# Decode block on one core: 24 of w2's rows on VectorE, wo's rows in pairs over two column groups, and TensorE's program on a 256 boundary

## Chip, core and metric

The kernel runs on one core of a Trainium2 chip. The metric is the device time of one execution in microseconds (us). Engines: TensorE (PE, with PEld for its weight loads), VectorE (DVE), ScalarE (ACT), GpSimd (POOL) and SyncE (SP), which issues nearly all DMA transfers. Sixteen DMA engines share every transfer.

## The reference

One token x of 1024 elements goes through a layer norm, then through two branches whose results are added to x:

```python
xn = layernorm(x)
# A: attention of 32 query heads over the last 4096 positions of 4 KV heads, head size 128
q = xn @ wq                                   # 1024 x 4096
p = softmax(q . k * 128**-0.5)                # 8 query heads share one KV head
A = (p . v) @ wo                              # 4096 x 1024
# B: MLP
h = gelu_tanh(layernorm(xn) @ w1 + b1)        # 1024 x 3584
B = h @ w2 + b2                               # 3584 x 1024
out = x + A + B
```

All inputs are bf16. Weights and the cached keys and values that are used come to 39.86 MB.

## The kernel before

All operations are written down in one plan (class `Plan`, lines 15 to 124) that works out the semaphore waits between engines; each engine then runs its operations in the order in which they were added. A read after a write waits on VectorE too, except on TensorE, where order is enough.

SyncE issues the transfers in this order: the keys (4 x 1 MB, line 181), wq in two halves (240), b1, x and b2 (318 to 320), w1 in two halves (359, 360), the values in three pieces (364), w2 in two pieces of 14 rows (401, 402), wo's rows 0 to 15 in one piece (446), and rows 16 to 31 in pieces of 8, 4, 2, 1 and 1 rows (`cuts`, 447 to 449). A "row" of w2 or wo is a tile of 128 partitions x 1024 columns: partition p holds row p*28+c of w2 or p*32+c of wo. Four SBUF slots of 32 KB per partition are reused: a transfer waits until the slot's earlier reader is done.

Stages: layer norms (272 to 308) on VectorE with small matmuls; transposition of the keys by VectorE (329) and ScalarE with VectorE (334, 338); q = xn @ wq (355) in four column groups; scores (395); softmax (399 to 428); w1 (375) in two halves around the softmax; gelu (434) and its transposition into hT (438), where hT[:, c, 0] is the column of weights for w2's row c; attention output (444), its head selection o_m, o_f, o_bf (451 to 455) and the column form o8 (457 to 460).

The end: w2's 28 rows are multiplied on TensorE into PSUM tile accw (467 to 473), each row as two matmuls of 512 columns in two column groups (the result's two halves lie on partitions 0 and 32). VectorE adds x + b2 (475). wo's rows 0 to 27, the bulk, go the same way into qo_ps (483 to 488). VectorE adds the w2 result in two pieces of 192 and 320 columns (491, 492). The last four rows go into acc2 in pieces of 320 and 192 columns (493 to 503); after row 30 four fp32 matmuls with one contraction row bring the 192-column piece of the bulk into that accumulation:

```python
        if c == CWO - 2:
            for half in range(2):
                pr = 32 * half
                mm32(acc_b[pr:pr + 1, :], ones_f[pr:pr + 1, 0:1], bulk_b[pr:pr + 1, :], False, False, ...)
```

VectorE adds the 320-column piece and converts (509), ScalarE converts the other (510), and two transfers write the output (512, 513).

TensorE's operations stand in a block of their own (lines 106 to 118) that ends with a branch back to its start which is never taken; `branch_hint` names that branch at the block's head. A second such branch at the start (lines 188 to 196) waits for x and leads to a block behind the program.

Of the kernel before, what the change touches and what calls it, by code (L numbers as in the profile page):

```python
# [7 lines left out]
FP32 = mybir.dt.float32  # L8
BF16 = mybir.dt.bfloat16
ACT = mybir.ActivationFunctionType  # L10
ALU = mybir.AluOpType
# [3 lines left out]
class Plan:  # L15
# [11 lines left out]
    def emit(self, done, never, inner):  # L27
        nc, ops = self.nc, self.ops
# [28 lines left out]
        for n, (eng, fn, r, w, dma, _) in enumerate(ops):  # L57
            c, mine = clock[eng], []
# [26 lines left out]
        def put(n):  # L85
            eng, fn, r, w, dma, _ = ops[n]
            lanes = {}
            for m in waits[n]:
                s, v = value[m]
                if id(s) not in lanes or lanes[id(s)][1] < v:  # L90
                    lanes[id(s)] = (s, v)
            for s, v in lanes.values():
                self.engines[eng].wait_ge(s, v)
            i = fn()
            if i is not None and n in value:
                i.then_inc(value[n][0], value[n][1] if dma is not None else 1)

        for n, o in enumerate(ops):
            if o[0] != "pe":
                put(n)  # L100
# [3 lines left out]
        only = [mybir.EngineType.PE]  # L104
        pe = nc.tensor
        pe_ops = [n for n, o in enumerate(ops) if o[0] == "pe"]
        pe.br("pe_main")
        nc.enter_bb("pe_main", valid_engines=only)
        back = pe.mark_branch_hint_location()
        for n in pe_ops:  # L110
            put(n)
        pe.br_eq(never, 1, "pe_main", "pe_last").branch_hint(back)
        nc.enter_bb("pe_last", valid_engines=only)
        pe.br("pe_end")
        nc.enter_bb("pe_far", parent=inner, valid_engines=only)
        pe.nop()
        pe.br("pe_go")
        nc.enter_bb("pe_end", valid_engines=only)
        pe.nop()
# [3 lines left out]
def kernel(  # L123
# [14 lines left out]
    nc = tc.nc  # L138
# [16 lines left out]
    TAIL = 4  # L155
    NA = 320
    NH = Fd // 8
# [4 lines left out]
    def sb(name, shape, dt):  # L162
        return nc.alloc_sbuf_tensor(name, shape, dt).ap()

    def ps(name, shape):
        return nc.alloc_psum_tensor(name, shape, FP32).ap()
# [5 lines left out]
    accw = ps("accw", [P, 512])  # L172
# [10 lines left out]

    x32 = sb("x32", [Hq, Hq], BF16)
# [4 lines left out]
    with tc.tile_critical():  # L189
        never = nc.tensor.alloc_register("pe_never")  # L190
        nc.tensor.reg_mov(never, 0)
        inner = nc.cur_bb
        far = nc.tensor.mark_branch_hint_location()
        nc.tensor.wait_ge(x_sem, 16)
        nc.tensor.br_eq(never, 1, "pe_far", "pe_go").branch_hint(far)
        nc.switch_bb("pe_go")
# [6 lines left out]
    def op(eng, fn, r=(), w=()):  # L203
        plan.add(eng, fn, r, w)

    def dma(eng, out_ap, in_ap, r=(), w=(), over=()):
        q = plan.engines[eng]
        plan.add(eng, lambda: q.dma_start(out=out_ap, in_=in_ap), r, w, True, over)  # L208

    def ldw(w_ap, pos, r):  # L210
        def go():
            with nc.discard():
                i = pe.ldweights(w_ap, tile_position=pos).ins
            return pe.add_instruction(mybir.InstLdweights(  # L214
                name=nc.get_next_instruction_name(), engine=i.engine, tile_size=(P, 32), tile_position=pos, ins=i.ins, outs=i.outs))
        op("pe", go, r, ())

    def mm(out_ap, w_ap, x_ap, start, stop, pos, r, w):
        def go():
            with nc.discard():  # L220
                i = pe.matmul(out_ap, lhsT=w_ap, rhs=x_ap, start=start, stop=stop, tile_position=pos).ins
            return pe.add_instruction(mybir.InstMatmult(  # L222
                name=nc.get_next_instruction_name(), engine=i.engine, start_tensor_calc=start, stop_tensor_calc=stop,
                tile_size=i.tile_size, tile_position=i.tile_position, ins=i.ins, outs=i.outs, ldweights=False))
        op("pe", go, r, w)
# [43 lines left out]
    op("dve", lambda: dve.memset(accw[0:33, :], 0.0), (), ("accw",))  # L269
# [43 lines left out]
    x2 = sb("x2", [33, 512], BF16)  # L313
    b2x = sb("b2x", [33, 512], BF16)
    b1x = sb("b1x", [P, 2 * NH], BF16)
    for name, t in (("x2", x2), ("b2x", b2x), ("b1x", b1x)):
        op("pool", lambda t=t: pool.memset(t, 0.0), (), (name,))
    dma("sp", b1x[0:97:32, :], B_b1.rearrange("(t n) -> t n", t=4), (), ("b1x",))
    dma("sp", x2[0:33:32, :], x_flat.rearrange("(t n) -> t n", t=2), (), ("x2",))
    dma("sp", b2x[0:33:32, :], B_b2.rearrange("(t n) -> t n", t=2), (), ("b2x",))  # L320

# [79 lines left out]
    dma("sp", slot[3][:, :14 * D].rearrange("p (r n) -> p r n", r=14), w2_v[:, 0:14, :], (), ("w20",), kt_srcs)  # L401
    dma("sp", slot[1][:, :14 * D].rearrange("p (r n) -> p r n", r=14), w2_v[:, 14:28, :], (), ("w21",), ("slot1",))
# [13 lines left out]
    op("dve", lambda: dve.tensor_scalar_mul(out=nmx, in0=mc_ps, scalar1=-scale), ("misc",), ("nmx",))  # L416
    l_loc = sb("l_loc", [P, 1], FP32)
# [17 lines left out]
    xb = sb("xb", [33, 512], FP32)  # L435
    op("dve", lambda: dve.tensor_tensor(out=xb, in0=x2, in1=b2x, op=ALU.add), ("x2", "b2x"), ("xb",))
    hT = sb("hT", [P, CW2, 32], BF16)
    op("dve", lambda: dve.transpose(out=hT, in_=h_sb.rearrange("p (d c) -> p c d", c=CW2)), ("h_sb",), ("hT",))

# [15 lines left out]
    op("dve", lambda: dve.tensor_copy(out=o_bf, in_=o_f), ("o_f",), ("o_bf",))  # L455
    o8_ps = misc[:, 160:192]
# [3 lines left out]
    op("dve", lambda: dve.tensor_copy(out=o8, in_=o8_ps), ("misc",), ("o8",))  # L460
    accf = qo_ps
    op("dve", lambda: dve.memset(accf, 0.0), (), ("qo",))
    acc_a, acc_b = acc2[:, 0, 0:NA], acc2[:, 1, 0:512 - NA]
    op("dve", lambda: dve.memset(acc2[:, :, 0:NA], 0.0), (), ("acc_a", "acc_b", "acc2"))


    for c in range(CW2):
        i, r = divmod(c, 14)
        wap = slot[3 - 2 * i][:, r * D:(r + 1) * D]
        for half in range(2):  # L470
            ldw(hT[:, c, 0:1], (0, 32 * half), ("hT",))
        for half in range(2):
            mm(accw[32 * half:32 * half + 1, :], hT[:, c, 0:1], wap[:, 512 * half:512 * half + 512], c == 0, c == CW2 - 1, (0, 32 * half), (f"w2{i}",), ("accw",))
    base = sb("base", [33, 512], FP32)
    op("dve", lambda: dve.tensor_tensor(out=base, in0=accw[0:33, :], in1=xb, op=ALU.add), ("accw", "xb"), ("base",))  # L475
    n_bulk = CWO - TAIL

    def wo_row(c):
        i, r = divmod(c, 16)
        key = "wo0" if i == 0 else f"wo1{max(a for a in cuts if a <= r)}"  # L480
        return wo_t[i][:, r, :], key

    for c in range(n_bulk):
        wap, key = wo_row(c)
        for half in range(2):
            ldw(o8[:, c:c + 1], (0, 32 * half), ("o8",))
            mm(accf[32 * half:32 * half + 1, :], o8[:, c:c + 1], wap[:, 512 * half:512 * half + 512],
               c == 0, c == n_bulk - 1, (0, 32 * half), (key,), ("qo",))
    bulk_b = sb("bulk_b", [33, 512 - NA], FP32)
    bulk_a = sb("bulk_a", [33, NA], FP32)  # L490
    op("dve", lambda: dve.tensor_tensor(out=bulk_b, in0=accf[0:33, NA:512], in1=base[:, NA:512], op=ALU.add), ("qo", "base"), ("bulk_b",))  # L491
    op("dve", lambda: dve.tensor_tensor(out=bulk_a, in0=accf[0:33, 0:NA], in1=base[:, 0:NA], op=ALU.add), ("qo", "base"), ("bulk_a",))
    for c in range(n_bulk, CWO):
        wap, key = wo_row(c)
        first, last = c == n_bulk, c == CWO - 1
        for half in range(2):
            ldw(o8[:, c:c + 1], (0, 32 * half), ("o8",))
        for half in range(2):
            pr, h0 = 32 * half, 512 * half
            mm(acc_a[pr:pr + 1, :], o8[:, c:c + 1], wap[:, h0:h0 + NA], first, last, (0, pr), (key,), ("acc_a",))  # L500
        for half in range(2):
            pr, h0 = 32 * half, 512 * half
            mm(acc_b[pr:pr + 1, :], o8[:, c:c + 1], wap[:, h0 + NA:h0 + 512], first, last, (0, pr), (key,), ("acc_b",))
        if c == CWO - 2:
            for half in range(2):
                pr = 32 * half
                mm32(acc_b[pr:pr + 1, :], ones_f[pr:pr + 1, 0:1], bulk_b[pr:pr + 1, :], False, False, ("ones_f", "bulk_b"), ("acc_b",), (pr, pr))
    res = sb("res", [33, 512], BF16)
    op("dve", lambda: dve.tensor_tensor(out=res[:, 0:NA], in0=acc_a[0:33, :], in1=bulk_a, op=ALU.add), ("acc_a", "bulk_a"), ("res_a",))  # L509
# [4 lines left out]
    plan.emit([len(plan.ops) - 2, len(plan.ops) - 1], never, inner)  # L514
# [30 lines left out]
```

## Time and profile before

Three runs: median 102.48 us (102.47 to 102.52). The profiled execution took 102.36 us, with a span of 100.44 us from the first to the last instruction.

| engine | busy us | share | instructions |
|---|---|---|---|
| PE | 45.8 | 46% | 351 |
| PEld | 15.2 | 15% | 263 |
| DVE | 47.8 | 48% | 60 |
| ACT | 30.5 | 30% | 28 |
| POOL | 5.4 | 5% | 19 |

The DMA queues: q1 carries SyncE's transfers (2498 packets, 39.86 MB), q10 ScalarE's, q8 and q14 the instructions of engines. The instruction packets inside the span: 16,384 bytes on q8 at 48.17 us (0.945 us long), 8,192 bytes on q14 at 60.14 (0.333), 16,384 bytes on q8 at 99.53 (0.959).

Each transfer ends, on each DMA engine, with a packet of 4 bytes. Their times show how far the sixteen engines are apart (us from the start of the span):

| transfer | first to fourteenth engine | fifteenth | last |
|---|---|---|---|
| wq, first half | 22.16 to 22.43 | 22.45 | 22.48 |
| w1, second half | 49.00 to 49.39 | 49.48 | 50.67 |
| w2, rows 0 to 13 | 67.32 to 67.81 | 68.56 | 69.12 |
| w2, rows 14 to 27 | 75.82 to 76.32 | 77.07 | 77.63 |
| wo, rows 0 to 15 | 85.54 to 86.03 | 86.78 | 87.35 |
| wo, rows 16 to 23 | 90.42 to 90.93 | 91.67 | 92.25 |
| wo, rows 24 to 27 | 92.91 to 93.41 | 94.16 | 94.74 |
| wo, rows 28 and 29 | 94.17 to 94.68 | 95.43 | 96.00 |
| wo, row 30 | 94.84 to 95.34 | 96.08 | 96.66 |
| wo, row 31 | 95.52 to 96.02 | 96.73 | 97.30 |

How to read the page: the slices divide the span into 40 parts; a digit is the busy share in tenths, PEclk the clock granted to TensorE in tenths of full speed. The chain of waits goes back from the last instruction to what released it; "DMA" in it is a transfer from issue to landing. In the groups, the columns are line, engine, operation, tiles and shapes, count, busy us, mean ns of one, and idle time before it with what ended that.

### The profile page before, as it was taken

Reading aid. Unit: us, or ns where it says so; the run is one execution under the profiler, and the core shown is the slowest. Engines: PE = TensorE matmul, PEld = TensorE weight load, DVE = VectorE, ACT = ScalarE, POOL = GpSimd, SP = SyncE. Lnnn points to the kernel's source line nnn. Section 1 sums busy time; section 2 is a strip of 40 time slices with the busy share of each in tenths; the row PEclk is TensorE's granted clock in tenths of the full one; section 3 lists DMA queues with packets and bytes.
Section 4 is the critical chain, followed back from the end, with each engine's and each line's share of the span. In section 5 each row is a group of like instructions: output and inputs, shape, how many; then the busy total and the mean of one; then the engine's idle time right before and its main releaser. Section 6 shows DMA issues by size and latency. Waiting matters only on the chain.

```text
span 100.4 us, 818 instructions
## 1 busy us (share of the span) xinstructions
PE 45.8 (46%) x351; PEld 15.2 (15%) x263; DVE 47.8 (48%) x60; ACT 30.5 (30%) x28; POOL 5.4 (5%) x19
## 2 busy tenths in 40 slices
PE   0032200008500940049958006998390890099981
PEld 0021200001000100011112002343130230034420
DVE  0164499999999999950263960001730002000021
ACT  0230000999998999900107510000000000000001
POOL 0262360000000000000000000000000000000000
PEclk9999999999995555555999955699999579556999
DMA  2899999999999999998899999999999999999920
GB/s 79 339 418 418 470 509 431 470 418 418 418 418 396 411 457 411 388 514 377 362 434 427 421 512 414 400 491 388 422 480 426 418 418 418 411 418 395 396 77 7
DMA packets 2551, 39.90 MB, mean 397 GB/s; under 512 B 362, under 2 KB 372, under 8 KB 756
## 3 DMA queue, kind: packets, MB, share of 16 engines
q1 hardware_dynamic: 2498, 39.86, 93.4%
q8 instruction: 2, 0.03, 0.1%
q10 hardware_dynamic: 50, 0.00, 0.0%
q14 instruction: 1, 0.01, 0.0%
HBM read 39.86 MB, written 0.00 MB: 397 GB/s over the span
## 4 chain that ended last, share of the span: by engine, by line
DMA 77%; PE 14%; SPq 2%; issue 1%; DVE 0%
DMA slot<-in_A_wq_dram 28%; DMA slot<-in_A_wo_dram 26%; DMA slot<-in_A_v_cache_dram 24%; PE qo_ps L222 9%; PE acc L222 5%; SPq L208 2%; DVE res L509 0%; PE acc L228 0%
## 5 line engine op out<-in xcount | busy, mean ns | idle before, releaser
L334 ACT COPY kT<-slot 32x1024 bf16<-32x1024 bf16 (+1 forms) x18 | 23.9, 1327 | 12.2 <-DVE slot L329 12.1
L329 DVE STREAM_TRANSPOSE slot<-slot 128x4096 bf16<-128x4096 bf16 x4 | 17.4, 4413 | 0.0
L222 PE MATMUL acc<-slot,xnT 128*1 128x512 bf16 x64 | 7.2, 626 | 18.0 <-DMA slot<-in_A_wq_dram 18.0
L510 ACT CAST res<-acc 33x192 bf16<-33x192 f32 x1 | 0.3, 313 | 40.2 <-PE acc L222 40.2
L338 DVE COPY kT<-slot 32x4096 bf16<-32x4096 bf16 x10 | 12.2, 1220 | 0.2
L222 PE MATMUL qo_ps<-slot,eTb 128*32 128x512 bf16 x32 | 8.8, 443 | 6.3 <-DMA slot<-in_A_v_cache_dram 6.3
L222 PE MATMUL qo_ps<-slot,o 128*1 128x512 bf16 x56 | 8.4, 463 | 4.9 <-DMA slot<-in_A_wo_dram 4.9
L222 PE MATMUL accw<-slot,hT 128*1 128x512 bf16 x56 | 8.1, 452 | 2.8 <-DMA slot<-in_B_w_dram 2.8
L491 DVE TENSOR_TENSOR bulk_b<-qo_ps,base 33x192 f32<-33x192 f32 x1 | 0.3, 349 | 12.6 <-PE qo_ps L222 12.6
L451 DVE TENSOR_TENSOR o_m<-qo_ps,grs 32x512 f32<-32x512 f32 x1 | 0.7, 679 | 10.2 <-PE qo_ps L222 10.2
L222 PE MATMUL sc_ps<-kT,qm 128*32 128x512 bf16 x32 | 5.2, 846 | 0.5 <-DVE qm L385 0.5
L214 PEld LDWEIGHTS <-o 128*1 128x1 bf16 x64 | 3.7, 95 | 11.3 <-issue 9.2
L214 PEld LDWEIGHTS <-eTb 128*32 128x32 bf16 x32 | 3.5, 109 | 11.2 <-issue 7.4
L475 DVE TENSOR_TENSOR base<-accw,xb 33x512 f32<-33x512 f32 x1 | 0.7, 683 | 9.3 <-PE accw L222 9.3
L214 PEld LDWEIGHTS <-xnT 128*1 128x1 bf16 x32 | 1.0, 121 | 22.9 <-issue 22.8
L214 PEld LDWEIGHTS <-hT 128*1 128x1 bf16 x56 | 2.7, 96 | 7.7 <-issue 5.6
L228 PE MATMUL qo_ps<-selq,q_sb 128*128 128x4 bf16 x8 | 0.4, 169 | 7.5 <-DVE q_sb L357 7.5
L222 PE MATMUL acc<-slot,yT 128*1 128x448 bf16 x64 | 3.4, 353 | 0.0
L228 PE MATMUL misc<-st,ones_f 128*128 128x1 f32 (+1 forms) x6 | 1.8, 362 | 3.2 <-DVE st L299 1.7
L400 DVE COPY sc<-sc_ps 128x512 f32<-128x512 f32 x1 | 0.7, 692 | 4.9 <-PE sc_ps L222 4.9
L228 PE MATMUL misc<-x,spread 32*128 32x8 bf16 x4 | 0.3, 168 | 5.9 <-POOL spread L249 5.9
L399 ACT COPY sc<-sc_ps 128x512 f32<-128x512 f32 x1 | 0.6, 586 | 7.2 <-PE sc_ps L222 7.2
(84 smaller groups left out, 36.8 us busy)
## 6 DMA issues: line engine op xcount, KB each, us to landing
slot<-in_B_w_dram SPq DMA_DIRECT2D x4, 3584.0 KB, 23.6
slot<-in_A_wq_dram SPq DMA_DIRECT2D x2, 4096.0 KB, 23.1
slot<-in_A_k_cache_dram SPq DMA_DIRECT2D x4, 1024.0 KB, 7.8
slot<-in_A_wo_dram SPq DMA_DIRECT2D x1, 4096.0 KB, 33.1
slot<-in_A_v_cache_dram SPq DMA_DIRECT2D x1, 2048.0 KB, 19.9
slot<-in_A_v_cache_dram SPq DMA_DIRECT2D x2, 1024.0 KB, 22.9
slot<-in_A_wo_dram SPq DMA_DIRECT2D x1, 2048.0 KB, 22.7
slot<-in_A_wo_dram SPq DMA_DIRECT2D x1, 1024.0 KB, 24.9
```

Source lines behind the costliest of these rows:

```text
L208: plan.add(eng, lambda: q.dma_start(out=out_ap, in_=in_ap), r, w, True, over)
L214: return pe.add_instruction(mybir.InstLdweights(name=nc.get_next_instruction_name(), engine=i.engine, tile_size=(P, 32), tile_position=pos ...
L222: return pe.add_instruction(mybir.InstMatmult(name=nc.get_next_instruction_name(), engine=i.engine, start_tensor_calc=start, stop_tensor_c ...
L228: op("pe", lambda: pe.matmul(out_ap, lhsT=w_ap, rhs=x_ap, start=start, stop=stop, tile_position=pos), r, w)
L329: op("dve", lambda s=s: dve.transpose(out=scr[:, s, :], in_=k2[:, s, :]), ("k0", "k1", "k2", "k3", "slot0"), (f"scr{s}",))
L334: op("act", lambda s0=s0, s1=s1, R=R, Cd=Cd: act.copy(out=kT[32 * Cd:32 * Cd + 32, R, s0:s1, :].rearrange("p s (c j) -> p (s c) j", j=32), ...
L338: op("dve", lambda R=R, Cd=Cd: dve.tensor_copy(out=kT[32 * Cd:32 * Cd + 32, R, :, :].rearrange("p s (c j) -> p (s c) j", j=32), in_=T3[32 ...
L399: op("act", lambda: act.copy(out=sc[:, 512:1024], in_=sc_ps[:, 1, :]), ("sc1",), ("scs1",))
L400: op("dve", lambda: dve.tensor_copy(out=sc[:, 0:512], in_=sc_ps[:, 0, :]), ("sc0",), ("scs0",))
L451: op("dve", lambda: dve.tensor_tensor(out=o_m, in0=o_all.rearrange("h (g d) -> h g d", g=Hkv), in1=grs.unsqueeze(2).to_broadcast([Hq, Hkv, ...
L475: op("dve", lambda: dve.tensor_tensor(out=base, in0=accw[0:33, :], in1=xb, op=ALU.add), ("accw", "xb"), ("base",))
L491: op("dve", lambda: dve.tensor_tensor(out=bulk_b, in0=accf[0:33, NA:512], in1=base[:, NA:512], op=ALU.add), ("qo", "base"), ("bulk_b",))
```

## The change

w2's rows 0 to 23 are multiplied and summed by VectorE: each is one `scalar_tensor_tensor` over 128 x 1024 (row times hT's column, plus a running fp32 sum), even rows into run[0], odd rows into run[1]. GpSimd puts x + b2 into run[0]'s first partition ahead of it, and VectorE adds run[1] to run[0] at the end. Rows 0 to 13 stand in VectorE's order ahead of o_m, o_f, o_bf; rows 14 to 23 behind. w2's first piece is loaded in pieces of 2, 4 and 8 rows.

TensorE multiplies w2's rows 24 to 27 and wo's rows 0 to 27 in pairs of rows: row c in column group 0 and row c+1 in column group 1, both halves of the columns, all into one PSUM tile (sc_ps, partitions 0 and 32), which VectorE clears after the softmax's maximum. o8 is copied by ScalarE instead of VectorE.

VectorE then adds this bulk to run[0]'s first 33 partitions (two instructions of 33 x 512). After row 29 fp32 matmuls with a column of 128 ones sum run[0] over its partitions into the last rows' accumulation, for all 1024 columns; rows 30 and 31 follow. VectorE's last instruction is now a copy.

TensorE's program gets an address alignment of 256 ahead of its first instruction; the block behind the program and the wait for x at the start go. VectorE's operations are put in a block of their own with a hinted branch back that is never taken, as TensorE's are. By the order of the instructions, TensorE has 494 weight loads and matmuls instead of 614.

```diff
+        own = [("dve", mybir.EngineType.DVE), ("pe", mybir.EngineType.PE)]
...
+        for e, kind in own:
+            nc.enter_bb(f"{e}_main", valid_engines=[kind])
+            back = self.engines[e].mark_branch_hint_location()
+            for n, o in enumerate(ops):
+                if o[0] == e:
+                    put(n)
+            self.engines[e].br_eq(never[e], 1, f"{e}_main", f"{e}_last").branch_hint(back)
+            nc.enter_bb(f"{e}_last", valid_engines=[kind])
+            self.engines[e].nop()
...
+    nc.tensor.addr_align(256, 0, 0)
...
-    with tc.tile_critical():
-        never = nc.tensor.alloc_register("pe_never")
-        nc.tensor.reg_mov(never, 0)
-        inner = nc.cur_bb
-        far = nc.tensor.mark_branch_hint_location()
-        nc.tensor.wait_ge(x_sem, 16)
-        nc.tensor.br_eq(never, 1, "pe_far", "pe_go").branch_hint(far)
-        nc.switch_bb("pe_go")
...
+    run = [sb(f"run{i}", [P, D], FP32) for i in range(2)]
...
+    op("pool", lambda: pool.tensor_tensor(out=run[0][0:1, :], in0=x2, in1=b2x, op=ALU.add), ("x2", "b2x"), ("run0",))
...
+    for a, b in ((0, 2), (2, 6), (6, 14)):
+        dma("sp", w2_t[0][:, a:b, :], w2_v[:, a:b, :], (), (f"w20{a}",), kt_srcs)
+    dma("sp", w2_t[1], w2_v[:, 14:28, :], (), ("w21",), ("slot1",))
...
+    op("dve", lambda: dve.memset(sc_ps[0:33, :, :], 0.0), (), ("sc0", "sc1", "bulk"))
...
+    op("dve", lambda: dve.tensor_copy(out=hTf, in_=hT[:, :, 0]), ("hT",), ("hTf",))
...
+    def running(c):
+        wap, key = w2_row(c)
+        if c == 1:
+            op("dve", lambda: dve.tensor_scalar_mul(out=run[1], in0=wap, scalar1=hTf[:, 1:2]), (key, "hTf"), ("run1",))
+        else:
+            t = run[c % 2]
+            op("dve", lambda: dve.scalar_tensor_tensor(out=t, in0=wap, scalar=hTf[:, c:c + 1], in1=t, op0=ALU.mult, op1=ALU.add),
+               (key, "hTf", f"run{c % 2}"), (f"run{c % 2}",))
...
+    op("dve", lambda: dve.tensor_tensor(out=run[0], in0=run[0], in1=run[1], op=ALU.add), ("run0", "run1"), ("run0",))
...
+    def bulk_rows(rows, w_of, cols, key, first, last):
+        for c in rows[::2]:
+            for u in range(2):
+                ldw(cols(c + u), (0, 32 * u), (key,))
+            for half in range(2):
+                for u in range(2):
+                    wap, wkey = w_of(c + u)
+                    mm(sc_ps[32 * u:32 * u + 1, half, :], cols(c + u), wap[:, 512 * half:512 * half + 512],
+                       first and c == rows[0], last and c == rows[-2], (0, 32 * u), (wkey,), ("bulk",))
...
+    bulk_rows(list(range(NB)), wo_row, lambda c: o8[:, c:c + 1], "o8", False, True)
+    for half in range(2):
+        op("dve", lambda half=half: dve.tensor_tensor(out=run[0][0:33, 512 * half:512 * half + 512], in0=bulk[:, half, :],
+                                                      in1=run[0][0:33, 512 * half:512 * half + 512], op=ALU.add), ("bulk", "run0"), (f"sum{half}",))
...
+        if c == CWO - 3:
+            for half in range(2):
+                for acc, a, b, akey in parts:
+                    pr, h0 = 32 * half, 512 * half
+                    mm32(acc[pr:pr + 1, :], ones_f[:, 0:1], run[0][:, h0 + a:h0 + b], False, False,
+                         ("ones_f", "run0", f"sum{half}"), (akey, "acc2"), (0, pr))
```

## The prediction, on record before the changed kernel ran

> **What bounds the kernel now.** I read the DMA row first, then the chain that ended last, then the end slice by slice. Slices of the page (2.5 us each):
>
> ```profile
> PEclk9999999999995555555999955699999579556999
> DMA  2899999999999999998899999999999999999920
> ```
>
> The DMA engines are full from about 3 us to 95 us. No compute saving inside that stretch can shorten it; only when the transfers end, and what is done after them, sets the time. The chain of waits, its last part (start us, us, what):
>
> ```profile
> 70.82 25.66 DMA slot<-in_A_wo_dram
> 96.49 0.10 issue
> 96.59 0.95 PE acc L222 x12
> 97.55 0.42 PE acc L228 x4
> 97.96 0.25 PE acc L222 x2
> 98.21 0.02 issue
> 98.23 0.48 DVE res L509
> ```
>
> The chain goes from wo's rows 28 and 29 through TensorE to the last add at 98.71 and the output. But the end of the transfers is ragged (stretch, length, busy by engine, granted clock, DMA share, GB/s):
>
> ```profile
> 95.25:95.50 0.25, 0.25 (x5) 0.11 (x5) 0.00 (x0) 0.00 (x0) 0.00 (x0) 1.00 1.04 385
> 95.75:96.00 0.25, 0.25 (x6) 0.12 (x4) 0.00 (x0) 0.00 (x0) 0.00 (x0) 1.00 0.37 131
> 96.25:96.50 0.25, 0.04 (x2) 0.00 (x0) 0.17 (x1) 0.00 (x0) 0.00 (x0) 1.00 0.17 66
> 97.00:97.25 0.25, 0.25 (x6) 0.06 (x2) 0.07 (x1) 0.00 (x0) 0.00 (x0) 1.00 0.06 25
> ```
>
> After 96 us only one or two of 16 engines still move data. The table of closing packets (above) says which: fourteen engines finish row 31 by 96.02, one at 96.73, one at 97.30. Up to 49.48 all sixteen closed a transfer within 0.48 us; the 1.3 us lag first shows at 50.67, right after an instruction fetch at 48.17, the 0.7 us lag after another at 60.14. Those two are in the queue table:
>
> ```profile
> q8 instruction: 2, 0.03, 0.1%
> q14 instruction: 1, 0.01, 0.0%
> ```
>
> Every transfer counts as landed when its last engine closes, and TensorE starts 0.51 to 0.59 us later (77.63 to 78.14, 87.35 to 87.92, 94.74 to 95.26, 96.00 to 96.59). So row 31 (97.30) could not start before about 97.85, and started at 97.89: the end hangs on the lagging engine, the four fp32 matmuls before it are hidden. Call that lag L: 1.3 us now.
>
> **The change, part by part.** Times are those of the profiled execution (102.36 us: span 100.44 and 1.92 around it); the median, 102.48, is 0.12 above it, and I add my difference to the median.
>
> *w2 on VectorE.* 48 of 56 matmuls of w2 leave TensorE (8.1 us busy, worth nothing: TensorE then waits for wo anyway) and 24 rows of 128x1024 come to VectorE, plus one sum. No row shows the operation. Nearest:
>
> ```profile
> L338 DVE COPY kT<-slot 32x4096 bf16<-32x4096 bf16 x10 | 12.2, 1220 | 0.2
> L405 DVE TENSOR_REDUCE m_loc<-sc 128x1 f32<-128x1024 f32 x1 | 1.2, 1220 | 0.4 <-ACT sc L399 0.4
> L475 DVE TENSOR_TENSOR base<-accw,xb 33x512 f32<-33x512 f32 x1 | 0.7, 683 | 9.3 <-PE accw L222 9.3
> ```
>
> Low end: a quarter of the copy's elements, 0.42 us with its 0.15 overhead. High end: the reduce over as many elements, 1.22, and 0.07 for a scalar read from a tile (0.23 against 0.16 on 128x8), 1.29. I take 1.20, nearest to the reduce. Rows 6 to 13 land at 67.81 + L + 0.62 (wait and smaller packets), then 8 rows, o_m/o_f/o_bf (1.96, 69.98 to 71.94), 10 rows and the sum: with L = 0.5, 68.9 + 19 x 1.20 + 1.96 = 93.7. It is needed at 95.8, so it is hidden up to 1.31 us a row. o_m now queues behind 14 rows: o_bf at 80.5, and with four matmuls and ScalarE's copy o8 at about 81.5, before wo's first row (87).
>
> *w2 in three more pieces, small DMAs.* Packets of 4, 8 and 16 KB cost 7, 5 and 3 ns more than at the 28 KB rate (159, 309, 611 against 1064 ns for 28 KB), 8 of each per engine: 0.12 us, all of it on the path. GpSimd's added memset and add, and the sc_ps clear (0.9, like acc2's 0.91, in the 1.31 us wait for ScalarE's exp) lie in slack of over 2 us ahead of hT.
>
> *wo in pairs of rows.* Half the weight loads, but two matmuls already overlap: 95.26 to 95.69 is four, 0.2155 us per pair of matmuls at full clock, 0.427 at half. Gain: 0. The bulk, 28 pairs, starts at 86.03 + L + 0.12 + 0.57 = 86.72 + L. With the clock granted at 91.97 as now and L = 0.5: 11.1 pairs at 0.427, 16.9 at 0.2155, streaming ends at 95.61. Rows 24 to 27 (93.41 + L + 0.12 + 0.52, four pairs) allow 95.41. So TensorE is the bound there.
>
> *The new end.* Two adds of 33x512 follow the bulk, where 33x192 and 33x320 did: VectorE starts 0.21 after the stream's end (as 96.33 after 96.12), second add 0.61 later, 0.68 long: 97.11. Then, after 0.07, a fp32 matmul over 128 partitions and 512 columns per column group. One pass of 192 columns takes 0.162 now (97.475 to 97.637), both groups side by side; two passes of 512 are 0.864: 98.04. Rows 30 and 31 queue behind it: 0.09 for the switch (as 97.80 to 97.89) and 0.43; the copy starts 0.34 after row 31's first part, as now, and takes 0.48. From the bulk's end that is 3.55 us; now it is 2.59. Sum for L = 0.5: 99.16 against 98.71, **+0.45**. If the fp32 passes were free or twice as long: -0.86 or +0.86; nothing else speaks for either.
>
> *Instruction fetches.* What this sum needs is L. [...] I take **L = 0.5**.
>
> [...]
>
> **Rivals.**
> 1. *No lag is left (L = 0).* [...] Place: the last engine's closing packets. Price: bulk streamed at 95.35, end 98.90, 102.67. It turns faster only where TensorE is not the bound either: clock granted by 90.2 (a stream started at 86.7 needs 3.5), bulk limited by rows 24 to 27 at 94.91, end 98.47, **102.24**. The decisive point is a bulk end before 94.95.
> 2. *The lag stays at 1.3* (the alignment doesn't do what I read): bulk held by its rows to 96.21, end 99.77, **103.55**. For: I have seen one fetch only, in one program.
> 3. *The clock comes late, or VectorE does.* The full clock was granted at 64.66, 81.73 and 91.97, apart by 5 and 3 times 3.413, whenever TensorE began. If that grid lies otherwise against the kernel and the grant comes at 93.6, the bulk ends at 96.41 for L = 0.5: **103.74**; now 0.6 us of that was hidden by row 31's landing, after the change nothing hides it. VectorE over 1.31 us a row costs 0.19 per 0.01. [...]
>
> **How the numbers follow.** Forecast, 102.9 (own range 102.7 to 103.1): 0.40. Rival 1: 0.27, half of it faster. Rival 2: 0.18. Rival 3: 0.15. About 0.2% (0.2 us) is what a measurement of this kernel can tell from no change. Faster 0.13 (half of rival 1), same 0.17 (its other half and the forecast's lower edge), slower 0.70. The range goes from rival 1's good end, 102.2, to 103.9, past rivals 2 and 3 but for the worst clock.
>
> **What would show it.** Closing packets of wo's last rows within 0.5 us of each other plus L; instruction packets gone from 48 and 60 us, or moved to the first 5. VectorE's rows at 1.1 to 1.3 us, the sum done by 94. The fp32 matmuls behind the second add, 0.86 long, and rows 30 and 31 behind them instead of waiting for DMA. Wrong if the fp32 matmuls don't run side by side over the column groups, if VectorE's rows are far slower or wait on each other, or if the outside 1.92 us change.

## The result: 102.97 us, and the profile after

The changed kernel takes 102.97 us (median of 20 runs, 102.44 to 104.27), the kernel before 102.34 (20 runs, 101.92 to 102.62): ratio 1.007, 95% interval 1.0049 to 1.0091. The one slow run among the 20, the 104.27, counts in the median and the range but not in the ratio, which compares the means of fast runs. By medians it is slower by 0.63 us; 102.9 was forecast, from a kernel before at 102.48. The profiled execution took 103.08 us: a span of 100.95, and 2.13 outside it (before: 100.44 and 1.92).

Slices of the page, 2.5 us each, clock and DMA:

```profile
PEclk9999999999999999999999999999855555556999
DMA  4799999999999999998999999998999999999900
```

The DMA engines are as full as before, and stop one slice earlier. The clock is at half from 72 us; full clock is granted at 92.71. The chain that ended last, its end (start us, us, what):

```profile
57.85 28.96 DMA slot<-in_A_wo_dram
86.85 9.10 PE sc_ps L214 x54
...
95.98 0.69 DVE run L496
...
96.71 1.02 PE acc L220 x4
97.74 0.14 PE acc L214
97.87 0.28 PE acc L220 x2
98.15 0.08 PE acc L214
98.23 0.10 PE acc L220
98.34 0.37 PE acc L214 x3
...
98.73 0.48 DVE res L515
```

In this profile no transfer stands in it after 86.85. wo's first piece releases the bulk, TensorE streams it without a pause, then follow the adds (L496), the fp32 matmuls (L220), the last rows among and behind them, and the copy. The same stretches at the end as were shown of before:

```profile
95.25:95.50 0.25, 0.25 (x6) 0.00 (x0) 0.00 (x0) 0.00 (x0) 0.00 (x0) 1.00 1.05 385
95.75:96.00 0.25, 0.25 (x8) 0.09 (x2) 0.02 (x1) 0.00 (x0) 0.00 (x0) 1.00 0.47 172
96.25:96.50 0.25, 0.12 (x4) 0.00 (x0) 0.25 (x1) 0.00 (x0) 0.00 (x0) 1.00 0.00 0
97.00:97.25 0.25, 0.25 (x2) 0.07 (x1) 0.25 (x1) 0.00 (x0) 0.00 (x0) 1.00 0.00 0
```

At 96.25 nothing moves any more: the straggling engines are gone. Row 31's fourteenth closing packet is at 96.14 and its last at 96.31 (before 96.02 and 97.30), wo's first piece has 86.17 and 86.35 (before 86.03 and 87.35): measured as the prediction measures it, L is 0.2. The queue table has one instruction fetch left:

```profile
q8 instruction: 1, 0.02, 0.1%
```

It stands at 1.93 us; those at 48 and 60 are gone. The instructions that touch run (duration min/median/max in ns, first and last start):

```profile
L445 DVE SCALAR_TENSOR_TENSOR run<-slot,hTf,run x23: 1266/1279/1286, 63.3 to 92.2; 128x1024 f32<-128x1024 bf16 x23
...
L220 PE MATMUL acc<-run,ones_f x8: 325/378/431, 96.7 to 98.0; 128*1 128x320 f32 x4, 128*1 128x192 f32 x4
L496 DVE TENSOR_TENSOR run<-sc_ps,run x2: 672/677/682, 96.0 to 96.6; 33x512 f32<-33x512 f32 x2
...
L469 DVE TENSOR_TENSOR run<-run x1: 1226/1226/1226, 93.5 to 93.5; 128x1024 f32<-128x1024 f32 x1
```

One of VectorE's rows takes 1.28 us and starts 1.196 us after the one before it: they overlap a little. w2's sum ends at 94.74, the first add could start at 95.98: 1.2 us to spare.

### The profile page after: what moved, and what is told of

The parts are those of the page before. It is cut to its first block, busy times and chain, and to the rows that moved or that the text cites. A ratio compares the mean times of both kernels' runs of the same rounds, so it can differ in the third digit from the quotient of the medians.

```text
span 101.0 us, 715 instructions
## 1 busy us (share of the span) xinstructions
PE 40.4 (40%) x307; PEld 11.1 (11%) x187; DVE 77.7 (77%) x81; ACT 30.7 (30%) x29; POOL 7.6 (8%) x19
## 4 chain that ended last, share of the span: by engine, by line
DVE 37%; DMA 29%; PE 22%; issue 3%; POOL 2%; ACT 1%; DVEq 0%; POOLq 0%
DMA slot<-in_A_wo_dram 29%; DVE slot L321 16%; PE sc_ps L214 15%; DVE kT L330 13%; PE misc L220 2%; PE acc L214 2%; DVE sel L301 2%; PE acc L220 1%; DVE m_loc L399 1%; DVE q_sb L349 1%; DVE run L496 1%; POOL spread L241 1%; ACT sc L391 1%; POOL st L281 1%; POOL st L296 1%
## 5 line engine op out<-in xcount | busy, mean ns | idle before, releaser
L445 DVE SCALAR_TENSOR_TENSOR run<-slot,hTf,run 128x1024 f32<-128x1024 bf16 x23 | 27.7, 1274 | 0.2 <-DVE hTf L433 0.2
L330 DVE COPY kT<-slot 32x4096 bf16<-32x4096 bf16 x10 | 14.0, 1402 | 0.2
L214 PE MATMUL sc_ps<-slot,o 128*1 128x512 bf16 x56 | 9.1, 502 | 5.0 <-DMA slot<-in_A_wo_dram 5.0
L214 PE MATMUL qo_ps<-slot,eTb 128*32 128x512 bf16 x32 | 7.1, 379 | 2.0 <-DMA slot<-in_A_v_cache_dram 2.0
L214 PE MATMUL sc_ps<-kT,qm 128*32 128x512 bf16 x32 | 6.1, 981 | 0.5 <-DVE qm L377 0.5
L214 PE MATMUL sc_ps<-slot,hT 128*1 128x512 bf16 x8 | 1.9, 620 | 10.1 <-DMA slot<-in_B_w_dram 10.1
L220 PE MATMUL qo_ps<-selq,q_sb 128*128 128x4 bf16 x8 | 0.4, 169 | 9.4 <-DVE q_sb L349 9.4
L313 POOL TENSOR_TENSOR run<-x,b2x 1x1024 f32<-1x1024 bf16 x1 | 2.3, 2251 | 18.6 <-DMA b2x<-in_B_b_dram 18.6
L206 PEld LDWEIGHTS <-o 128*1 128x1 bf16 x36 | 2.0, 100 | 12.9 <-issue 12.4
L220 PE MATMUL misc<-st,ones_f 128*128 128x1 f32 (+1 forms) x6 | 1.8, 362 | 3.1 <-DVE st L290 1.7
L220 PE MATMUL misc<-x,spread 32*128 32x8 bf16 x4 | 0.3, 168 | 6.4 <-POOL spread L241 6.4
```

Of the source, the lines that this page charges most:

```text
L206: return pe.add_instruction(mybir.InstLdweights(name=nc.get_next_instruction_name(), engine=i.engine, tile_size=(P, 32), tile_position=pos ...
L214: return pe.add_instruction(mybir.InstMatmult(name=nc.get_next_instruction_name(), engine=i.engine, start_tensor_calc=start, stop_tensor_c ...
L220: op("pe", lambda: pe.matmul(out_ap, lhsT=w_ap, rhs=x_ap, start=start, stop=stop, tile_position=pos), r, w)
L313: op("pool", lambda: pool.tensor_tensor(out=run[0][0:1, :], in0=x2, in1=b2x, op=ALU.add), ("x2", "b2x"), ("run0",))
L330: op("dve", lambda R=R, Cd=Cd: dve.tensor_copy(out=kT[32 * Cd:32 * Cd + 32, R, :, :].rearrange("p s (c j) -> p (s c) j", j=32), in_=T3[32 ...
L445: op("dve", lambda: dve.scalar_tensor_tensor(out=t, in0=wap, scalar=hTf[:, c:c + 1], in1=t, op0=ALU.mult, op1=ALU.add), (key, "hTf", f"run ...
```

## The experiments

**Theory**: the changed kernel's end is one chain, the bulk (limited by TensorE and its clock), two adds, the fp32 sum, the last rows, the copy. The fetches' lag was worth about what this longer tail costs, so little moves. **Rivals**: the end still hangs on the transfers; or the program's layout did it all, and nothing of the lag has to do with w2. Each was timed beside the kernel before on the same chip: 102.44 us with the first four below, 102.30 with the next four measured, 102.31 with the last four; the changed kernel's ratio is the one above, against 102.34. So kernels of different groups are best compared by their ratios.

| kernel | median us (range) | ratio to before, 95% | median span | median outside |
|---|---|---|---|---|
| before (beside the second four) | 102.30 (101.99-102.78) | 1 | 100.5 | 1.83 |
| changed | 102.97 (102.44-104.27) | 1.0049-1.0091 | 100.85 | 2.12 |
| no alignment | 103.36 (103.24-104.24) | 1.0078-1.0129 | 101.6 | 1.79 |
| no hint for VectorE | 103.02 (102.82-103.37) | 1.0045-1.0079 | 100.85 | 2.15 |
| no fp32 sum | 101.54 (101.16-102.13) | 0.9897-0.9949 | 99.55 | 1.81 |
| six matmuls ahead | 102.95 (102.80-103.42) | 1.0039-1.0075 | 100.5 | 2.54 |
| before, new layout | 102.25 (101.87-102.57) | 0.9974-1.0007 | 100.4 | 1.83 |
| late addition | 102.91 (102.40-104.06) | 1.0026-1.0092 | 100.8 | 2.10 |
| 24 rows | 101.84 (101.49-102.84) | 0.9942-0.9992 | 99.95 | 1.82 |
| 24 rows, matmuls ahead | 102.06 (101.84-103.74) | 0.9965-1.0020 | 100.3 | 1.81 |
| unsplit end alone | 102.85 (102.46-104.29) | 1.0035-1.0081 | 101.0 | 1.82 |
| 24 rows, longer program | 102.18 (101.75-103.33) | 0.9972-1.0011 | 100.1 | 2.13 |
| 20 rows, late addition | 101.74 (101.40-102.11) | 0.9932-0.9965 | 100.0 | 1.79 |
| 20 rows, late, matmuls ahead | 102.02 (101.53-102.29) | 0.9946-0.9981 | 99.9 | 1.83 |

"Outside" is a run's time less its span. Medians of the parts need not add up to the median of the whole.

### Without the alignment

```diff
-    nc.tensor.addr_align(256, 0, 0)
```

> The changed kernel without the alignment of TensorE's program; all else as it is. Theory (the lag of one DMA engine comes from an instruction fetch of TensorE inside the loaded stretch, and the alignment is what moved it to 1.9 us): a 16,384 byte packet on q8 comes back near 48 to 53 us, the last engine closes wo's row 31 near 97.3 instead of 96.31 while the fourteenth stays near 96.0, wo's first piece closes near 87.3, and the time is 0.4 to 0.7 us above the changed kernel (near 103.5, about 1.1 above the kernel before). Rival A (one DMA engine is slow for a reason of its own and merely happened not to be in the changed kernel's profile): closings as in the changed kernel, time within 0.2 of it. Rival B (alignment acts on TensorE's own stalls): gaps between TensorE's matmuls where no semaphore holds it, with unchanged closings.

103.36 us. The fetch is back inside the stream, 16,384 bytes at 50.54; row 31's last closing packet is at 97.50 with the fourteenth at 96.20, wo's first piece closes at 87.55 instead of 86.35. The end of the chain:

```profile
70.51 26.18 DMA slot<-in_A_wo_dram
96.68 0.04 issue
96.72 0.60 PE acc L213 x8
97.32 0.95 PE acc L219 x4
98.27 0.14 PE acc L213
98.40 0.27 PE acc L219 x2
```

A transfer that lands at 96.68 is in it again, as in the kernel before. The median span is 0.75 us longer than the changed kernel's, with L 1.1 us larger (1.3 for 0.2). The time is only 0.39 longer, because the time outside the span is 0.33 shorter (1.79 for 2.12). This is rival 2 of the prediction, made to happen: with one fetch in the full stream, one DMA engine closes wo's first piece 1.2 us later than in the changed kernel, and row 31 1.3 us behind the fourteenth. TensorE's matmuls go on through the fetch (50.54 to 51.50); it is the transfers that come late, and the span is the 0.75 us longer.

### Without VectorE's hinted block

```diff
-        own = [("dve", mybir.EngineType.DVE), ("pe", mybir.EngineType.PE)]
+        own = [("pe", mybir.EngineType.PE)]
...
-            if o[0] not in ("dve", "pe"):
+            if o[0] != "pe":
```

> The changed kernel with VectorE's operations in the common block, without the hinted branch. Theory: an 8,192 byte packet on q14 comes back near 58 to 66 us, one engine then closes every transfer about 0.7 us after the fourteenth (row 31 near 96.8), the bulk starts about 0.4 us later; time 0.1 to 0.4 above the changed kernel (near 103.2). Rival (VectorE's fetch costs nothing, or the hint has nothing to do with it): no such packet or no such lag, time within 0.1 of the changed kernel.

103.02 us, 0.05 above the changed kernel. VectorE's fetch is back (8,192 bytes at 68.89), so the hint does remove it. Row 31 closes at 97.13, but that lag isn't VectorE's: in this profile TensorE's fetch came at 2.82 us instead of 1.93, and one engine was behind long before 68.89 (w2's rows 6 to 13 close on fifteen engines by 68.17, on the last at 68.98). After VectorE's fetch a second engine is behind it: wo's first piece closes on fourteen by 86.40, on the last two at 87.00 and 87.20. In time nothing is seen: full clock was granted at 91.20 here, 1.5 us earlier than in the changed kernel's profile, and the bulk that started 0.9 later ended only 0.2 later. What this fetch costs stays unresolved.

### Without the fp32 sum

```diff
-        if c == CWO - 3:
+        if False:
```

> The changed kernel without the fp32 matmuls over 128 partitions after row 29: the output then lacks x, b2, w2's 24 rows on VectorE and the bulk of wo. Theory (the end is the two adds and these matmuls, 3.44 us behind the bulk, not the landing of the data): rows 30 and 31 start when they land, row 31 near 96.9, VectorE's copy ends near 97.7 instead of 99.21; time 1.5 below the changed kernel, near 101.4 and 0.9 below the kernel before: the floor that the transfers without a lag leave. Rival (the end is bound by the output and what follows it, or by the transfers all the same): less than 0.5 won.

101.54 us: 1.43 below the changed kernel, 1.3 of it in the span (100.85 to 99.55) and 0.3 outside, by medians. The end:

```profile
69.17 27.86 DMA slot<-in_A_wo_dram
97.02 0.04 issue
97.06 0.31 PE acc L214 x2
97.38 0.02 issue
97.40 0.48 DVE res L515
```

Here row 31's landing (closing at 96.54) ends the kernel, as it doesn't in the changed one. So the wait for the adds and the fp32 matmuls add 1.3 us behind the point that the transfers would allow: the rival that the transfers still bind the changed kernel falls.

### Six unused matmuls ahead of the bulk

```diff
+        if c == 15:
+            ldw(hT[:, 27, 0:1], (0, 0), ("hT", "run1"))
+            for _ in range(6):
+                mm(qo_ps[0:1, :], hT[:, 27, 0:1], w2_t[1][:, 13, 0:512], True, True, (0, 0), ("w21",), ("qo",))
```

> The changed kernel with six matmuls added that nothing uses, behind VectorE's 16th row (from about 84 us), so that TensorE is busy before wo's first rows land. Theory (the bulk is bound by TensorE at half clock until 92.7, and the grant falls on a grid that doesn't follow the kernel): full clock is granted between 87 and 91, the bulk's stream ends near 95.1 (rows 24 to 27 landing) instead of 95.77, time 0.4 to 0.7 below the changed kernel (near 102.4), and the runs lie closer together than 102.44 to 104.27. Rival (the bulk waits for wo's rows whatever the clock): bulk's end unchanged, time within 0.2 of the changed kernel.

102.95 us, no gain. But the profile did what was meant: full clock granted at 89.43 instead of 92.71, last copy ended at 98.72 instead of 99.21, span 100.455. What came in its place is outside the span: 2.54 us in the median. A 16,384-byte fetch stands at 99.45 in that profile and ends at 100.74, after the span's last instruction. That led to the experiment with a longer program, below.

### The kernel before with the new layout

The kernel before, with the changed kernel's blocks, alignment and hints, and without the wait for x at the start:

```diff
+        own = [("dve", mybir.EngineType.DVE), ("pe", mybir.EngineType.PE)]
...
+    nc.tensor.addr_align(256, 0, 0)
...
-        far = nc.tensor.mark_branch_hint_location()
-        nc.tensor.wait_ge(x_sem, 16)
```

> The kernel before (all of w2 on TensorE, its own end) with the changed kernel's program layout alone: TensorE's program on the 256 boundary, the waiting block at the start gone, VectorE in a block of its own with a hinted branch. [...] Rival (the alignment alone removes the lag): the last closing packets within 0.5 us of each other, the time near 101.7, and w2 need not have moved to VectorE for that.

102.25 us: nothing gained. The fetch at 48 went to 1.93 us, VectorE's is gone, and a new one came at 57.26 (16,384 bytes). wo's first piece closes on fifteen engines by 86.23 and on the last at 87.40: the lag is there. So the layout alone doesn't do it. That moving w2 to VectorE helps the stream by shortening TensorE's program (625 instructions against 503 from the aligned start), and by nothing else, is what this pair suggests; it isn't shown, since the longest changed kernel that was run has 510.

### GpSimd's addition later

```diff
-    op("pool", lambda: pool.tensor_tensor(out=run[0][0:1, :], in0=x2, in1=b2x, op=ALU.add), ("x2", "b2x"), ("run0",))
...
+    op("pool", lambda: pool.tensor_tensor(out=run[0][0:1, :], in0=x2, in1=b2x, op=ALU.add), ("x2", "b2x", "q_sb0"), ("run0",))
```

> The changed kernel with GpSimd's addition of x and b2 moved behind the q matmuls' copy instead of running at about 33 us beside VectorE's key copies. Theory (the addition slows VectorE's copies beside it, which makes the scores, the softmax and hT late, and nothing at the end depends on that): all ten key copies take 1.22 us, the hT copy comes 1.5 to 2 us earlier, VectorE's sum of w2 is done near 93 instead of 94.7, and the time stays within 0.2 of the changed kernel. Rival (VectorE's late sum holds up the end): the time falls by over 0.3.

102.91 us: hidden, as the theory had it. VectorE's key copies (min/median/max ns, first and last start) and then the addition, in the changed kernel:

```profile
L330 DVE COPY kT<-slot x10: 1217/1220/3048, 31.0 to 43.9; 32x4096 bf16<-32x4096 bf16 x10
```

```profile
L313 POOL TENSOR_TENSOR run<-x,b2x x1: 2251/2251/2251, 33.2 to 33.2; 1x1024 f32<-1x1024 bf16 x1
```

and the copies with the addition later:

```profile
L329 DVE COPY kT<-slot x10: 1215/1220/1223, 31.8 to 42.9; 32x4096 bf16<-32x4096 bf16 x10
```

The one long copy began at 33.49, beside the addition (33.20 to 35.45), and ended 1.08 us after it. Later, all ten take 1.22, hTf is done at 61.95 instead of 63.18, and w2's sum at 94.19 instead of 94.74, both less early than expected; the end doesn't care. In this profile the last engine is 0.65 us behind at row 31, and wo's rows 28 and 29, landed at 96.24, stand in the chain again: their matmuls run to 96.89, the first add to 96.75.

### 24 rows of bulk, an unsplit end

```diff
-    NB = 28
+    NB = 24
...
+    acc = acc2[:, 0, :]
+    parts = [(acc, 0, 512, "acc")]
...
+    op("dve", lambda: dve.tensor_copy(out=res[0:1, :], in_=acc[0:1, :]), ("acc",), ("res_a",))
+    op("act", lambda: act.copy(out=res[32:33, :], in_=acc[32:33, :]), ("acc",), ("res_b",))
```

> The changed kernel with wo's rows 24 to 27 behind the fp32 sum instead of ahead of it: the bulk is 24 rows, the last eight rows (24 to 31) go into one PSUM bank without the 320/192 split, VectorE copies one output half and ScalarE the other, each output transfer waits for its own half. Theory (the end is a chain that starts at the bulk's end: two adds, fp32 matmuls, last rows, copy; TensorE waits idle for VectorE's adds): with four rows fewer ahead of the adds the chain starts earlier, and the four rows moved behind the fp32 matmuls fill TensorE while it is at full clock. Expected: VectorE's adds 0.9 us earlier or as early as the clock allows, last copy ends near 98.7 (changed kernel 99.21), time 102.3 to 102.6, no more than 0.2 from the kernel before. Rival (the end is bound by the last transfers, as in the kernel before): row 31 lands at 96.3 either way, nothing moves, 103.0.

101.84 us, faster than both kernels (than before by 0.1 to 0.6%), and better than expected. The edit does a little other than the expectation says: rows 24 to 27 stand behind the bulk that VectorE adds, but the fp32 sum still follows row 29, so they run beside the adds and ahead of the fp32 matmuls. The adds started 0.89 us earlier (95.09 for 95.98), the last copy ended at 98.77. Its chain:

```profile
70.25 25.87 DMA slot<-in_A_wo_dram
96.12 0.04 issue
96.16 0.59 PE acc L214 x4
96.76 0.86 PE acc L220 x4
97.62 0.45 PE acc L214 x4
98.06 0.02 issue
98.09 0.68 DVE res L515
```

VectorE's adds are no longer in it: they end at 96.37, while TensorE works on rows 28 and 29, which landed at 96.12. The fp32 sum is now 0.86 us in one stretch. What the expectation had too high was the time outside: 1.82, not the changed kernel's 2.12.

### The unsplit end alone

The changed kernel's 28 rows of bulk, with the end of the version above:

```diff
-    NB = 24
+    NB = 28
```

> One half of the version with 24 rows: the changed kernel's 28 rows of bulk stay, the last four rows go into one PSUM bank without the 320/192 split, VectorE copies one output half and ScalarE the other, each output transfer waits for its own half. TensorE's program gets 16 instructions shorter than the changed kernel's. [...] Rival (the gain came from the unsplit end): span near 100.3, time near 101.9.

102.85 us, 0.95 above the rival's 101.9. Its median span, 101.0, is no shorter than the changed kernel's 100.85, and the time outside is 1.82. So the shorter span comes from the four rows that moved, and the unsplit end gives the 0.3 outside only.

### 24 rows and a longer program

Twelve unused weight loads behind the last matmul, which bring TensorE's program from the aligned start on from 491 instructions to 503, the changed kernel's length:

```diff
+    for _ in range(12):
+        ldw(o8[:, 31:32], (0, 0), ("o8",))
```

> The version with 24 rows, and twelve unused weight loads at the end of TensorE's program, behind the last matmul, so that the program is as long as the changed kernel's. [...] Rival (the time outside the span has to do with the number of output waits or with nothing in the program): it stays at 1.8, time near 101.85.

102.18 us; span 100.1, outside 2.13 (24 rows: 99.95 and 1.82). The program's length alone brings the 0.3, without any change to the work. Over the changed kernel and its versions that are aligned: 487 to 500 instructions, 1.79 to 1.83 outside; 503, 2.10 to 2.15; 510, 2.54. The aligned kernel before, with 625, has 1.83. So it isn't the longer the program the more, and the cause is not shown. This version's profile has a fetch at the end (16,384 bytes at 101.96, behind the span's end at 100.15) and 2.50 outside, and so has that of the six unused matmuls (2.69). But at 503 the profiles of the changed kernel and of the late addition have no fetch at the end, with 2.1 outside, and at 500 the profile of the next version has one, at 102.64.

### Matmuls ahead of 24 rows

As the 24 rows, with eight unused matmuls behind VectorE's row 15:

```diff
+        if c == 15:
+            ldw(hT[:, 27, 0:1], (0, 0), ("hT", "run1"))
+            for _ in range(8):
+                mm(qo_ps[0:1, :], hT[:, 27, 0:1], w2_t[1][:, 13, 0:512], True, True, (0, 0), ("w21",), ("qo",))
```

> As bulk24q, and eight unused matmuls on TensorE behind VectorE's row 15 (they write a PSUM tile that nothing reads later), so that TensorE is busy in the idle time before wo's first rows. Theory (the clock's grant sets how fast the bulk streams): granted near 89.4 instead of 92.7, the bulk's end and the last copy 0.4 us earlier than bulk24q, VectorE's copy ends near 98.3; if the time outside the span stays near 2.0 the time is 101.9 to 102.3, faster than both kernels. Rival (as the six unused matmuls behaved in the changed kernel): the span gets shorter by 0.4 and the time outside it longer by 0.5, the time does not move against bulk24q.

102.06 us: not faster than without them. Full clock was granted at 90.50, but VectorE's sum ended only at 95.57 (hTf was 0.8 us later in that profile, which is of one of the longer runs, 103.28), and the adds waited for it until 95.67. The profile with the longer program shows the same without unused matmuls: granted at 89.70, the bulk streamed by 93.73, VectorE's sum done at 94.98 and the adds from 95.08. With an early clock VectorE's rows are the bound, so the next version takes the late addition along.

### 20 rows of bulk, late addition

Against the 24 rows:

```diff
-    NB = 24
+    NB = 20
...
-        if c == CWO - 3:
+        if c == CWO - 5:
```

and GpSimd's addition behind the q matmuls, as above.

> The version with 24 rows, with two more steps: 20 rows of bulk with the fp32 sum behind row 27, and GpSimd's addition of x and b2 behind the q matmuls. Theory (in that version TensorE waits 1 us for VectorE's adds and VectorE's own sum is done just before them): VectorE's sum is done near 94.2, the adds near 95.5, TensorE streams rows 20 to 27 meanwhile and the fp32 sum follows without a wait; the last copy starts 0.2 to 0.4 earlier, time 101.5 to 101.7. Rival (the last row's landing plus its wait is the bound by now): no gain, 101.85.

101.74 us, ratio to before 0.9949 (0.9932 to 0.9965): faster than both kernels. Against the 24 rows (101.84, measured at another time) the difference isn't resolved, and the two steps weren't run apart. The chain:

```profile
55.32 31.86 DMA slot<-in_A_wo_dram
...
87.22 7.00 PE sc_ps L214 x40
94.22 1.73 PE acc L214 x16
95.95 0.86 PE acc L220 x4
96.81 0.88 PE acc L214 x8
...
97.71 0.68 DVE res L516
```

From the bulk's start TensorE never waits: the adds (94.26 to 95.54) lie beside rows 20 to 27. One microsecond of both kernels, first the changed one, then this one (busy PE, PEld, DVE, ACT, POOL, clock, DMA share, GB/s):

```profile
96.00:97.00 1.00, 0.66 (x10) 0.10 (x3) 1.00 (x2) 0.00 (x0) 0.00 (x0) 1.00 0.04 14
```

```profile
96.00:97.00 1.00, 1.00 (x8) 0.26 (x6) 0.00 (x0) 0.00 (x0) 0.00 (x0) 1.00 0.06 23
```

In the changed kernel VectorE is busy there and TensorE partly idle; here TensorE works all of it. Row 31's matmuls begin at 97.29, 0.65 us after its last closing packet (96.64).

### Matmuls ahead of 20 rows

As above, with four unused matmuls behind VectorE's row 15:

```diff
-            for _ in range(8):
+            for _ in range(4):
```

> As the version with 20 rows and the late addition, with four unused matmuls on TensorE behind VectorE's row 15 (they write a PSUM tile that nothing reads later). Theory (the clock's grant still sets how fast the rows stream): granted in one of the windows near 89 to 91, the last copy 0.2 earlier than without them where the grant came after 91 there, time 101.3 to 101.6. Rival (row 31's landing bounds the end, or four matmuls are too few to bring a grant): no difference.

102.02 us: no gain. Full clock was granted at 91.62, against 92.36 without them, but the fetch came at 2.78 us and left row 31's last engine 0.88 us behind the fifteenth (97.12 for 96.24), and the bulk began 0.47 later. Row 31's matmuls began at 97.61, 0.49 after its last packet and 0.17 later than the pace of the rows before them: in this profile its landing is the bound, as the rival had it. What the earlier clock alone would bring can't be told from this pair; unused matmuls brought no time in any of three kernels.

## Why the prediction was right

The number hit, and the path to it held: the transfers lose their lag, the new end costs more than that gains, TensorE and its clock bound the bulk. But several of its terms were off and cancelled, which is luck, and two of its own signs of being wrong came: the fp32 matmuls didn't run side by side, and the time outside the span changed.

**What bounds the kernel: right.** The lag from the fetch was worth about what I took from it. Without the alignment it came back, 1.1 us larger, and the span grew by 0.75 us; rival 2 and the forecast were 0.65 apart for a lag 0.8 larger. At 48.17 TensorE had started 164 of its 614 loads and matmuls; why the fetch came just then, no run shows.

**The lag L: 0.2, taken 0.5.** The fetch did move to 1.93 us, and VectorE's did go. No run of this kernel shows the 0.5, which was my estimate; its profile has 0.2. The bulk began at 86.85, forecast 87.22; with L = 0.2 the forecast's own sum gives 86.92. So L was nearer to rival 1's 0 than to the forecast.

**The clock: 92.71, taken 91.97, and that gave the gain back.** By the forecast's own rule (13.7 pairs at 0.427, 14.3 at 0.2155) the stream ends at 95.79; it ended at 95.77, forecast 95.61. With the grant at 91.97 the same rule gives 95.42: the smaller lag and the later clock cancelled, and that they did is luck. The stretches up to the grant and behind it (columns as above):

```profile
85.88:89.30 3.42, 2.45 (x12) 0.39 (x6) 3.42 (x4) 0.00 (x0) 0.00 (x0) 0.50 1.01 431
89.30:92.71 3.41, 3.41 (x18) 0.52 (x8) 3.41 (x4) 0.00 (x0) 0.00 (x0) 0.50 0.97 408
92.71:96.12 3.41, 3.41 (x36) 0.68 (x16) 2.14 (x3) 0.00 (x0) 0.00 (x0) 1.00 0.92 358
```

A stretch with TensorE busy for 2.45 of 3.42 us brought no grant, a full one did; in the profile of the 24 rows with the longer program 2.76 of 3.41 (86.28 to 89.70) was enough. In the changed kernel's profile the clock changed at 51.75, 72.23 and 92.71, 20.48 apart, six times the 3.413 of before. Where the grid lies differs from run to run: in these kernels' profiles the grant came between 89.43 and 93.37. That nothing hides this after the change, as rival 3 said, fits the spread: the changed kernel's 20 spans go from 100.3 to 101.6, those of before (35 runs) from 100.2 to 100.9. How much of it is the clock and how much the lag of the early fetch, which also varies (below), isn't shown.

**VectorE's rows: right, 1.196 against 1.20.** That they are hidden: right, though with 1.2 us to spare instead of 2.1, because the sum ended at 94.74 and not at 93.7.

**The slack ahead of hT: wrong.** I put GpSimd's added work into "slack of over 2 us". It was GpSimd's slack; VectorE had none there. hT's transposition ended at 62.96, 3.1 us later than before (59.83). Of that the copy held up by the addition is 1.83; the scores took 0.87 longer, with full clock from 51.75 on (before from 47.60); and VectorE's first long work, the key transposes, began 0.4 later. With the addition later, hTf is done at 61.95 and, in the version with 20 rows, at 60.64 instead of 63.18. Only the cover behind it kept this from the end.

**The tail: 3.44, forecast 3.55.** The adds came 0.21 and 0.61 later as forecast. What I hadn't seen is that each column group waits for its own add: group 0's fp32 matmuls ran from 96.71, group 1's from 97.31, staggered and not side by side, and the last ended at 98.34. That cost nothing: group 1's start 0.06 after the second add and issue for 0.86, as the sum has it, and group 0's rows 30 and 31 run beside them, so that the copy starts 0.56 after their last pass instead of 0.64. Free of the fp32 part I put the time at 0.86 less; it was 1.43 less (1.3 of it span), because the wait for the adds goes with it.

**Outside the span: not foreseen.** I assumed 1.92 unchanged; it rose by 0.3 (medians 1.83 to 2.12), through the length of TensorE's program. By medians the 0.63 us are 0.35 of span and 0.29 outside. The span's part was forecast as 0.45, 0.10 too much, and the forecast stood on 102.48 for before, 0.14 above its 20-run median. These two make up for nearly all of the 0.29: that the number came out at 102.97 for 102.9 is luck in this part.

**wo in pairs, gain 0**: the pairs take 0.427 at half clock and 0.2155 at full, as in the forecast; no run tried the old order by itself. Nor was the cost of w2's smaller pieces tried.

## What to carry to other kernels

When a full stream of transfers sets the time, look for what shares its engines: here the last engine was 1.3 us behind at row 31 with an instruction fetch of 16,384 bytes at 50.54 us, and 0.2 with it at 1.93, and the program's alignment decided between the two. A sum that one engine hands to another at the end belongs ahead of work that the other still has: moving eight rows behind the hand-over, with a shorter program and the late addition, turned a loss of 0.63 us into a gain of 0.57 (by medians). After such a change look again at what the old bound was hiding, here the clock's grant.

## What the runs showed of the hardware that was not expected

- **GpSimd held up VectorE.** A 1x1024 addition on one partition took 2.25 us, and a VectorE copy that started 0.29 us after it took 3.05 instead of 1.22. Moved behind the copies (44.91 to 47.03) it had only two VectorE casts beside it, which took 0.18 us as without it. The long copy ended 1.08 us after the addition, where a copy takes 1.22 alone. How the one holds up the other is not shown.
- **A fetch at 1.93 us wasn't always free either.** It took between 1.03 and 1.72 us beside the first transfers, and the longer it took the further the last engine was behind the fifteenth at row 31: 0.0 us where it took 1.12 and 1.13, 0.15 and 0.2 at 1.20, 0.3 at 1.32, 0.5 at 1.44, 0.65 at 1.62 and 1.72. In two profiles it came at 2.8 us instead and left an engine 1.0 us behind at the first transfers (6.66 for 5.69, 6.62 for 5.62).
- **The time outside the span changed with the program**: 1.8 us at 487 to 500 instructions, 2.1 at 503 and 2.5 at 510.
